# Two activations placed behind copies, a table loaded in three parts, and two small loads placed later, in an S4D and spectral-filter kernel

## The chip, the cores and the metric

One core of a Trainium2 chip runs the whole kernel. The metric is the device time of one execution in microseconds; the median of several runs counts. Data lie in the chip's HBM; a transfer (DMA) brings them into the on-chip memory of 128 partitions, and matmuls write to PSUM, from where another engine has to copy them away. The engines are TensorE (PE; its weight loads appear as PEld), VectorE (DVE), ScalarE (ACT), GpSimd (POOL) and SyncE (SP), which here only issues transfers. Each works through its own queue of instructions.

## The reference

The input x has 2048 positions and 640 channels. Branch a is a state-space convolution over the positions, branch b a two-dimensional spectral filter, and a gate worked out from x mixes them.

```python
dt = exp(log_dt)                                   # one per channel
A = -exp(log_A_real) + 1j * A_imag                 # 640 x 128
C = (C_real + 1j * C_imag) * dt[:, None]
P = exp((A * dt[:, None])[:, :, None] * pos)
K = 2.0 * einsum("dn,dnl->dl", C, P).real          # a filter per channel
y = irfft(rfft(u_t, 2 * L) * rfft(K, 2 * L))[:, :, :L]
a = y + u * D_skip
X = rfft2(x) * (w_r + 1j * w_i)
b = irfft2(X)
g = sigmoid((x * gate_w).sum(-1))
out = g * a + (1 - g) * b
```

## The kernel before

All Fourier transforms over the positions are two steps of small matmuls. The **first step** (`stage1`) takes 32-point transforms: four channels' matmuls fill one PSUM buffer, and a copy brings it to a tile `t1`. The **second step** (`stage2`) multiplies `t1` with a table `w2` (33 matrices of 128 x 128) and fills one PSUM buffer per pair of frequencies; a copy brings that to `ut`. There are three PSUM buffers for both steps, and four `ut` tiles, each of which holds two copies of the second step and is then written to a buffer `u_d` in HBM (line 455).

Phase A (`phase_a`) does this for u in four quarters of the channels (`c` 0 to 3). Each quarter is loaded in two halves (line 412, three buffers), the first step runs over 2 x 20 columns, and between come small matmuls with the gate's weights `z` (lines 417, 442). Then the second step makes 17 copies. The copies (line 405) are ScalarE's until a marked matmul, `T.pin`, in quarter 1; after it they are VectorE's.

Phase P (`phase_p`) makes the parameters of the filter K. From log_dt it works out dt on tiny tiles. From C it takes the larger and the smaller of the two parts, their quotient `q` (lines 308 to 313), its Arctan on ScalarE (line 316), the phase `ph` out of that (317 to 329), and from `q` again the logarithm of the magnitude, with Ln on ScalarE (line 338) and what follows (339 to 342). The activation Exp of line 344 and what GpSimd makes of it give the decay; GpSimd also makes the angle `th`. Each result is split into three bf16 parts (`parts`), and these are written to two buffers in HBM: `par_d[0]` for angles and phases, with constant rows from the table `t_one` beside them, and `par_d[1]` for decays and magnitudes.

Phase B (`phase_b`) builds K in 40 steps. It reads the parameters back (line 660), multiplies `par_d[1]`'s with a constant `rm` (line 670, in the helper `mags`, followed by Exp), `par_d[0]`'s with `rp` (line 680, followed by Sin), and sums the products over the 128 states (line 723). Its first matmuls may not stand before `T.pin`.

What sets the order: the phases are generators that yield from time to time. `body` advances phase P to its first yield, phase A to its first, then phase P to its end, then phase A until `T.pin` exists; from there `merge` interleaves phase A, and after it the spectral branch and phase C (`ga`), with phase B (`gl`). The instructions are then put in order, engine by engine, by a planner that goes by this order and by when it takes an instruction to be ready; so an instruction can stand ahead of one that was traced earlier. `tc.issue_after(x)` makes what is traced inside it stand behind x on x's engine, without a wait on another engine. The planner also puts the waits between engines. Transfers are issued from the queue of the engine that is named: `nc.sync` is SP, `G` is GpSimd, `nc.scalar` is ScalarE.

The skip weights `T.dsk` (D_skip, line 423, four rows) are first used in phase C, at line 782.

Of the kernel before, what the change touches and what calls it, by code (L numbers as in the profile page):

```python
# [12 lines left out]
AF = mybir.ActivationFunctionType  # L13
# [11 lines left out]
NP = 33  # L25
# [170 lines left out]
def body(tc, A, out):  # L196
    nc = tc.nc
    T = Ctx()
    with ExitStack() as top:
        dram = top.enter_context(tc.tile_pool(name="dram", bufs=1, space=DRAM))  # L200
        T.u_d = dram.tile([4, 128, 17, 2, 160], F32, name="u_d")
        T.s3e_d = dram.tile([4, 32, 64, 160], F32, name="s3e_d")
        T.s3_d = dram.tile([4, 64, 64, 160], F32, name="s3_d")
        T.k_d = dram.tile([4, 128, 40, 64], F32, name="k_d")
        T.par_d = [dram.tile([8, 4, 32, 5, N], BF, name="par_d0"), dram.tile([8, 16, 6, 5, N], BF, name="par_d1")]
        cst = top.enter_context(tc.tile_pool(name="cst", bufs=1))
        c1 = cst.tile([128, A["t_c1"].shape[1]], F32, name="c1")
        for x in (slice(0, 256), slice(256, c1.shape[1])):
            nc.scalar.dma_start(c1[:, x], A["t_c1"][:, x])
        o = 0  # L210

        def take(n):
            nonlocal o
            o += n
            return c1[:, o - n:o]

        T.e1 = [take(128), take(128)]
        T.e3, T.e3e, T.id, T.one = take(64), take(128), take(128), take(32)
        T.sg = [take(1), take(1)]
        T.hpi = take(1)  # L220
        T.w2 = cst.tile([128, NP, 128], F32, name="w2")
        T.gate = cst.tile([128, 2, 16], F32, name="gate")
        T.dsk = cst.tile([128, 4, 40], F32, name="dsk")
        T.pin = None
        with ExitStack() as cctx:
            def left():
                with ExitStack() as ctx:
                    T.bc = ctx.enter_context(tc.tile_pool(name="b_c", reuse_waits="tile", bufs=1))
                    T.rm = T.bc.tile([96, 1536], BF, name="rm")
                    T.rp = T.bc.tile([128, 2560], BF, name="rp")  # L230
                    yield from phase_p(tc, A, T)
                    yield 0.0
                    yield from phase_b(tc, A, T, ctx)

            ga, gl = chain(phase_a(tc, A, T), phase_c(tc, A, T, cctx)), left()
            next(gl)
            next(ga)
            next(gl)
            while T.pin is None:
                next(ga)  # L240
            merge((194.0, ga), (76.8, gl))
            phase_d(tc, A, T, cctx, out)


def phase_p(tc, A, T):

    nc = tc.nc
    V, G, S = nc.vector, nc.gpsimd, nc.scalar
    with ExitStack() as ctx:
# [11 lines left out]
        lar, ai, cr, ci = tn("lar"), tn("ai"), tn("cr"), tn("ci")  # L261
        for t, nm in ((cr, "cr_l"), (ci, "ci_l"), (ai, "ai_l"), (lar, "la_l")):
            nc.sync.dma_start(t[:, :, :], A[nm])
        nc.sync.dma_start(T.par_d[0][:, :, 24:32], A["t_one"])

        x, kf, r, h = t5("x"), t5("kf"), t5("r"), t5("h")
        V.tensor_scalar(out=x[:, :], in0=ld[:, :], scalar1=-87.0, scalar2=88.0, op0=ALU.max, op1=ALU.min)
        V.tensor_scalar(out=kf[:, :], in0=x[:, :], scalar1=1.0 / LN2, scalar2=MAGIC, op0=ALU.mult, op1=ALU.add)
# [31 lines left out]
        with tc.issue_after(ins.ins):  # L300
            G.dma_start(T.rm[:, :], A["t_rm"])
            G.dma_start(T.rp[:, :], A["t_rp"])
        G.tensor_tensor(out=th[:, :, :], in0=th[:, :, :], in1=w2[:, :, :], op=ALU.subtract)
        G.tensor_scalar(out=th[:, :, :], in0=th[:, :, :], scalar1=0.5, scalar2=-0.5, op0=ALU.min, op1=ALU.max)

# [7 lines left out]
        V.tensor_tensor(out=q[:, :, :], in0=q[:, :, :], in1=w[:, :, :], op=ALU.mult)  # L313
        V.tensor_tensor(out=ab[:, :, :], in0=ab[:, :, :], in1=ar[:, :, :], op=ALU.is_gt)
        ph, y = tn("ph"), tn("y")
        S.activation(ph[:, :, :], q[:, :, :], AF.Arctan)
        V.tensor_scalar(out=ph[:, :, :], in0=ph[:, :, :], scalar1=1.0 / (2 * math.pi), scalar2=None, op0=ALU.mult)
        V.tensor_scalar(out=y[:, :, :], in0=ph[:, :, :], scalar1=-2.0, scalar2=0.25, op0=ALU.mult, op1=ALU.add)
        V.tensor_tensor(out=y[:, :, :], in0=y[:, :, :], in1=ab[:, :, :], op=ALU.mult)
# [15 lines left out]
        V.tensor_tensor(out=w[:, :, :], in0=ff, in1=ff, op=ALU.mult)  # L335
        V.tensor_tensor(out=q[:, :, :], in0=q[:, :, :], in1=q[:, :, :], op=ALU.mult)
        V.scalar_tensor_tensor(out=q[:, :, :], in0=q[:, :, :], scalar=1.0, in1=w[:, :, :], op0=ALU.add, op1=ALU.mult)
        S.activation(q[:, :, :], q[:, :, :], AF.Ln)
        V.tensor_scalar(out=y[:, :, :], in0=ex[:, :, :], scalar1=-126.0, scalar2=LN2, op0=ALU.add, op1=ALU.mult)
        V.scalar_tensor_tensor(out=q[:, :, :], in0=q[:, :, :], scalar=0.5, in1=y[:, :, :], op0=ALU.mult, op1=ALU.add)  # L340
        V.tensor_tensor(out=q[:, :, :], in0=q[:, :, :], in1=bc(ld), op=ALU.add)
# [33 lines left out]
def phase_a(tc, A, T):  # L375
    nc = tc.nc
    V, G, S, P = nc.vector, nc.gpsimd, nc.scalar, nc.tensor

    with ExitStack() as ctx:
        def pool(name, bufs):  # L380
            return ctx.enter_context(tc.tile_pool(name=name, side="right", reuse_waits="tile", bufs=bufs))


        au = pool("a_u", 3)
        ap = pool("a_p", 2)
        ta = [pool("a_t0", 1)]
        a1 = pool("a_1", 4)
        ta.append(pool("a_t1", 1))
        ac = pool("a_c", 1)
        ps = ctx.enter_context(tc.tile_pool(name="a_ps", side="right", reuse_waits="tile", bufs=3, space=PSUM))  # L390
        gw = ac.tile([128, 4, 40], F32, name="gw")
        lg = ac.tile([128, 8, 64], F32, name="lg")
        lr = ac.tile([128, 64], F32, name="lr")


        V.memset(lg[:, :, :], 0.0)
        V.memset(T.dsk[:, :, :], 0.0)
        z = lg.rearrange("p x a -> p (x a)")
        p = ps.tile([128, 512], F32, tag="ps", name="p_w")
        for _ in range(2):  # L400
            P.matmul(p[:, :], z[:, 0:128], z, start=True, stop=True)

        def copy(dst, src):

            (V.tensor_copy if T.pin else S.copy)(dst, src)  # L405

        us = []

        def load(c, h):
            us.append(au.tile([128, 20, 64], F32, tag="u", name="u"))  # L410
            for q0, q1 in ((0, 6), (6, 20)) if c + h == 0 else ((0, 20),):
                nc.sync.dma_start(us[-1][:, q0:q1, :], A["u_l"][c, :, 20 * h + q0:20 * h + q1])

        def weights(c, h):

            z = ap.tile([128, 20, 32], F32, tag="z", name="z")
            G.tensor_tensor(out=z[:, :, :], in0=T.one.unsqueeze(1).broadcast_to([128, 20, 32]),  # L417
                            in1=gw[:, c, 20 * h:20 * h + 20].unsqueeze(2).broadcast_to([128, 20, 32]), op=ALU.mult)
            return z

        nc.scalar.dma_start(gw[:, :, :], A["gw_l"])
        for r in range(4):
            nc.sync.dma_start(T.dsk[32 * r:32 * r + 1, :, :], A["ds_l"][r:r + 1])
        load(0, 0)
        load(0, 1)
        zs = [weights(0, 0), weights(0, 1)]
        for c in range(4):
            t1 = ta[c % 2].tile([128, 16, 160, 2], F32, tag="t1", name="t1")
            t1v = t1.rearrange("p x d y -> p d x y")
            for h in range(2):  # L430
                u, z = us.pop(0), zs.pop(0)
                if c + h == 0:
                    yield 0.0
                    nc.sync.dma_start(T.w2[:, :, :], A["t_w2"].rearrange("p (k m) -> p k m", m=128))
                if c < 3:
                    load(c + 1, h)
                yield from stage1(nc, ps, T.e1, lambda q: u[:, q, :], 20, t1v[:, 80 * h:80 * h + 80], copy)

                p = ps.tile([128, 64], F32, tag="ps", name="p_g")
                for q in range(20):  # L440
                    x = 32 * (q % 4)
                    P.matmul(p[x:x + 32, :], z[:, q, :], u[:, q, :], start=q < 4, stop=q > 15)
                    if q % 4 == 3:
                        yield 0.15
                S.copy(lg[:, 2 * c + h, :], p[:, :])
                if c < 3:
                    zs.append(weights(c + 1, h))
            for pr in range(0, 17, 2) if c < 3 else (8, 10, 12, 14, 16, 0, 2, 4, 6):
                n = min(2, 17 - pr)
                nl = 128 if pr < 16 else 64  # L450
                ut = a1.tile([128, 2, 2, 160], F32, tag="ut", name="ut")
                for i in range(n):
                    pv, ins = stage2(nc, ps, T.w2, t1, pr + i, 1)
                    copy(ut[:nl, i:i + 1], pv)
                nc.sync.dma_start(T.u_d[c, :nl, pr:pr + n], ut[:nl, :n])
                if (c, pr) == (1, 8):
                    T.pin = ins
                yield 0.55 * n


        p = ps.tile([128, 64], F32, tag="ps", name="p_g")
        V.tensor_reduce(out=lr[:, :], in_=lg.rearrange("p x a -> p a x"), axis=mybir.AxisListType.X, op=ALU.add)
        for r in range(4):
            P.matmul(p[32 * r:32 * r + 32, :], T.one, lr[:, :], start=True, stop=True)
        for r, x in enumerate((slice(31, 15, -1), slice(32, 48), slice(15, None, -1), slice(48, 64))):
            V.tensor_copy(T.gate[32 * r:32 * r + 32, 0, :], p[32 * r:32 * r + 32, x])
# [556 lines left out]
```

## Time and profile before

| what | value |
|---|---|
| median of three runs | 594.21 us (591.97 to 594.76) |
| the profiled execution | 594.76 us, span 592.8 us |
| TensorE busy | 544.7 us, 92% |
| VectorE busy | 459.0 us, 77% |
| ScalarE busy | 324.8 us, 55% |
| GpSimd busy | 263.0 us, 44% |
| moved by DMA | 100.94 MB, mean 170 GB/s |

The span is the time from the first to the last instruction of the profiled execution; the run's own time is a little longer. A row of the timeline reads: start and duration in us, engine, source line, operation, output and inputs, form, count; in brackets the time for which the engine was idle before it and what ended that. Rows of equal instructions are merged, and their duration is that of all of them. An engine's name with a q (SPq) is its queue's own instruction, such as the issue of a transfer. A row of waits reads: engine, operand and line, what it waited for, and then the total in us, the number of waits, and the longest. A float32 matmul appears as two records. A row of transfers gives the operand, queue, count, size of one, and the time from the end of its issue to its landing. A row of windows gives the stretch, its length, the busy time of PE, PEld, DVE, ACT and POOL with the number of instructions, the clock granted to TensorE as a share of full speed, the DMA engines' busy share and GB/s.

### The profile page before, as it was taken

How to read it: one execution, taken by the hardware profiler on the slowest of the kernel's cores; microseconds unless marked ns; L12 is line 12 of the kernel's file. 1: busy time of each engine (PE TensorE's matmuls, PEld its weight loads, DVE VectorE, ACT ScalarE, POOL GpSimd, SP SyncE). 2: the span in 40 equal slices, each digit the busy share in tenths (PEclk: the TensorE clock that was granted, in tenths of full speed). 3: DMA queues.
4: the chain of work that ended last, by engine and by line, in shares of the span. 5: the costliest groups of instructions: out<-in, count | busy, mean ns of one | idle time of the engine just before them, and what ended most of it. 6: DMA issues, size and time to landing. Idle time of an engine off the chain costs nothing. (4 is left out here: it accounts for less than half of the span.)

```text
span 592.8 us, 16600 instructions
## 1 busy us (share of the span) xinstructions
PE 544.7 (92%) x7084; PEld 400.4 (68%) x7084; DVE 459.0 (77%) x713; ACT 324.8 (55%) x579; POOL 263.0 (44%) x267
## 2 busy tenths in 40 slices
PE   9388899999979999999899999899889999999975
PEld 7278556757665666675667675665778978887751
DVE  5993379688779989979969968958469596785955
ACT  4346666465826776777587878487632423232120
POOL 3972055053345616336406316217335256647533
PEclk9879999999979999999799999999999999999989
DMA  8757512317532340234140223012695989989787
GB/s 270 301 212 232 186 55 79 137 26 270 216 101 73 93 151 11 69 127 156 58 120 11 66 69 121 24 50 91 229 389 177 336 283 335 336 250 315 262 255 272
DMA packets 47409, 100.94 MB, mean 170 GB/s; under 512 B 3460, under 2 KB 32920, under 8 KB 45544
## 3 DMA queue, kind: packets, MB, share of 16 engines
q1 hardware_dynamic: 24936, 68.06, 33.4%
q10 hardware_dynamic: 20080, 22.52, 12.0%
q0 software_dynamic: 2320, 9.31, 4.6%
q8 instruction: 55, 0.90, 0.6%
q14 instruction: 18, 0.15, 0.1%
HBM read 60.55 MB, written 39.65 MB: 169 GB/s over the span
## 5 line engine op out<-in xcount | busy, mean ns | idle before, releaser
L370 PE MATMUL p_s<-t,w 128*64 128x160 f32 x1056 | 93.3, 316 | 14.8 <-ACT ut L405 8.7
L370 PEld LDWEIGHTS p_s<-t,w 128*64 128x64 f32 x1056 | 78.8, 140 | 25.3 <-ACT ut L405 9.5
L672 ACT ACTIVATE e<-p_e 128x512 f32<-128x512 f32 x120 | 68.8, 603 | 26.4 <-PE p_e L670 24.6
L709 POOL TENSOR_TENSOR y<-e,sc 128x512 f32<-128x512 f32 x40 | 51.8, 1295 | 62.6 <-ACT sc L694 35.9
L691 DVE TENSOR_SCALAR aq<-p_p 128x512 int32<-128x512 int32 x80 | 53.8, 684 | 22.5 <-PE p_p L680 22.1
L723 PEld LDWEIGHTS p_k<-x,y 128*32 128x32 f32 x2560 | 44.6, 111 | 36.5 <-issue 33.4
L589 PE MATMUL p_eo<-td,pmt 107*128 107x321 f32 x204 | 66.9, 442 | 0.3 <-ACT pmt L541 0.3
L680 PE MATMUL p_p<-rp,par 128*128 128x512 bf16 x240 | 65.6, 381 | 0.5 <-ACT sx L696 0.3
L723 PE MATMUL p_k<-x,y 128*32 128x64 f32 x2560 | 60.7, 225 | 1.2 <-POOL z L417 0.7
L358 ACT COPY t<-p_s 128x512 f32<-128x512 f32 x40 | 24.8, 624 | 64.7 <-PE p_s L357 45.2
L710 POOL TENSOR_TENSOR y<-e,sc 128x512 f32<-128x512 f32 x40 | 53.8, 1345 | 0.0
L706 DVE TENSOR_TENSOR x<-e,cx 128x1024 f32<-128x1024 f32 x40 | 48.5, 1212 | 2.4 <-ACT cx L697 2.4
L831 DVE TENSOR_TENSOR ma<-p_s,us 128x640 f32<-128x640 f32 (+1 forms) x36 | 28.2, 783 | 27.8 <-PE p_s L370 16.4
L589 PEld LDWEIGHTS p_eo<-td,pmt 107*128 107x128 f32 x204 | 36.9, 189 | 17.4 <-issue 4.3
L670 PE MATMUL p_e<-rm,par 96*128 96x512 bf16 x120 | 43.6, 386 | 5.0 <-ACT sx L696 3.7
L859 PE MATMUL p_i<-t,w 128*64 128x160 f32 x528 | 44.4, 304 | 4.0 <-POOL t L837 3.7
L357 PE MATMUL p_s<-c,kt 128*64 128x128 f32 x640 | 43.3, 274 | 3.4 <-POOL kt L782 2.1
L357 PEld LDWEIGHTS p_s<-c,kt 128*64 128x64 f32 x640 | 38.9, 136 | 10.4 <-issue 6.1
L357 PE MATMUL p_s<-c,u 128*64 128x128 f32 x640 | 43.0, 281 | 2.0 <-ACT ut L405 1.7
L859 PEld LDWEIGHTS p_i<-t,w 128*64 128x64 f32 x528 | 38.3, 139 | 8.4 <-POOL t L837 4.3
L357 PEld LDWEIGHTS p_s<-c,u 128*64 128x64 f32 x640 | 36.3, 139 | 11.3 <-issue 6.2
L837 POOL TENSOR_TENSOR t<-mb 64x320 f32<-64x320 f32 (+1 forms) x36 | 29.8, 828 | 28.3 <-DVE t L837 27.8
(157 smaller groups left out, 1069.0 us busy)
## 6 DMA issues: line engine op xcount, KB each, us to landing
u_d<-ut SPq DMA_DIRECT2D x32, 320.0 KB, 3.0
us<-u_d ACTq DMA_DIRECT2D x16, 640.0 KB, 6.5
s_d<-s ACTq DMA_DIRECT2D x15, 640.0 KB, 9.5
t<-s_d SPq DMA_DIRECT2D x14, 640.0 KB, 4.3
ww<-in_w_l SPq DMA_DIRECT2D x8, 642.0 KB, 3.8
ue<-u_d SPq DMA_DIRECT2D x8, 640.0 KB, 5.2
k_d<-kt SPq DMA_DIRECT2D x4, 1280.0 KB, 6.4
kt<-k_d SPq DMA_DIRECT2D x8, 640.0 KB, 6.4
```

What stands on the lines that cost most here:

```text
L357: nc.tensor.matmul(p[64 * ri:64 * ri + 64, j, :], src(i + j), e1[ri], start=True, stop=True)
L370: ins = nc.tensor.matmul(p[64 * j:64 * j + 64, i, 160 * ri:160 * ri + 160], w2[:, x, 64 * ri:64 * ri + 64], t1[:, x // 2 if x < 32 else K0 ...
L589: P.matmul(p[:, :E], st.pmt[:DC, c, w, j, :], tv[:DC, w, c, :], start=c == 0, stop=c == 2)
L670: P.matmul(p[:, :], pars[1][t], rm[:, c:c + 512], start=True, stop=True)
L672: st.exp = S.activation(ef[:, c:c + 512], p[:, :], AF.Exp)
L680: P.matmul(p[:, :], pars[0][t], w, start=i == 0, stop=i == 2)
L691: V.tensor_scalar(out=af[:, c:c + 512].bitcast(I32), in0=r.p[c][:, :].bitcast(I32), scalar1=0x7FFFFFFF, scalar2=None, op0=ALU.bitwise_and)
L706: V.tensor_tensor(out=x[:, 0].rearrange("p d (h j) -> p d h j", h=2), in0=e[:, :, 0:64].rearrange("p d (h j) -> p d h j", h=2), in1=cx.uns ...
L709: G.tensor_tensor(out=y[:, 1], in0=e[:, :, 64:96], in1=sc[:, 0], op=ALU.mult)
L710: G.tensor_tensor(out=y[:, 0], in0=e[:, :, 64:96], in1=sc[:, 1], op=ALU.mult)
L723: P.matmul(st.pb[32 * r:32 * r + 32, o, :], y[:, ri, 4 * qq + JR[r], :], x[:, ri, 4 * qq + JR[r], :], start=t % 2 + qq + 1 - ri == 0, stop ...
L859: T.mm = P.matmul(p[x:x + 64, i // 2, 160 * (i % 2):160 * (i % 2) + 160], T.w3[:, k0 + h + i, x:x + 64], t2[:, h + i, :], start=True, stop ...
```

## The change

- Arctan (line 316) is traced after six copies of the second step and stands behind the sixth on ScalarE; Ln (line 338) is traced after sixteen copies and stands behind the sixteenth. What phase P does after each of them is traced later with it. To that end, phase A keeps its copies of the second step in a list `T.cps`, phase P yields twice more, and `body` advances the two in turn.
- The table `w2` comes in three loads of eleven matrices each, in place of one.
- The four rows of skip weights are issued after the first load for quarter 1, in place of before the loads of quarter 0.
- The constant rows `t_one` go to `par_d[0]` from GpSimd's queue, behind the loads of `rm` and `rp`, in place of from SyncE's.

```diff
-        T.pin = None
+        T.pin, T.cps = None, []
...
             next(gl)
             next(ga)
+            for n in (6, 15):
+                next(gl)
+                while len(T.cps) < n:
+                    next(ga)
             next(gl)
             while T.pin is None:
                 next(ga)
...
             nc.sync.dma_start(t[:, :, :], A[nm])
-        nc.sync.dma_start(T.par_d[0][:, :, 24:32], A["t_one"])
...
             G.dma_start(T.rp[:, :], A["t_rp"])
+            G.dma_start(T.par_d[0][:, :, 24:32], A["t_one"])
...
-        S.activation(ph[:, :, :], q[:, :, :], AF.Arctan)
+        yield 0.0
+        with tc.issue_after(T.cps[-1].ins):
+            S.activation(ph[:, :, :], q[:, :, :], AF.Arctan)
...
-        S.activation(q[:, :, :], q[:, :, :], AF.Ln)
+        yield 0.0
+        with tc.issue_after(T.cps[-1].ins):
+            S.activation(q[:, :, :], q[:, :, :], AF.Ln)
...
-            (V.tensor_copy if T.pin else S.copy)(dst, src)
+            return (V.tensor_copy if T.pin else S.copy)(dst, src)
...
         nc.scalar.dma_start(gw[:, :, :], A["gw_l"])
-        for r in range(4):
-            nc.sync.dma_start(T.dsk[32 * r:32 * r + 1, :, :], A["ds_l"][r:r + 1])
         load(0, 0)
         load(0, 1)
...
                 if c + h == 0:
                     yield 0.0
-                    nc.sync.dma_start(T.w2[:, :, :], A["t_w2"].rearrange("p (k m) -> p k m", m=128))
+                    for x in range(0, NP, 11):
+                        nc.sync.dma_start(T.w2[:, x:x + 11, :], A["t_w2"].rearrange("p (k m) -> p k m", m=128)[:, x:x + 11, :])
                 if c < 3:
                     load(c + 1, h)
+                if c + h == 0:
+                    for r in range(4):
+                        nc.sync.dma_start(T.dsk[32 * r:32 * r + 1, :, :], A["ds_l"][r:r + 1])
...
                     pv, ins = stage2(nc, ps, T.w2, t1, pr + i, 1)
-                    copy(ut[:nl, i:i + 1], pv)
+                    T.cps.append(copy(ut[:nl, i:i + 1], pv))
```

## The prediction

> **What bounds the kernel now.** I read the page first.
>
> ```profile
> span 592.8 us, 16600 instructions
> PE 544.7 (92%) x7084; PEld 400.4 (68%) x7084; DVE 459.0 (77%) x713; ACT 324.8 (55%) x579; POOL 263.0 (44%) x267
> PE   9388899999979999999899999899889999999975
> ```
>
> TensorE is busy for 92% of the span, and its order is laid down in advance. So time is lost where TensorE stands still, and a stall taken out moves all that follows. The first hole is the second slice (14.8 to 29.6 us, three tenths busy), where the change works. Next come the waits of the first 64 us, for TensorE and ScalarE.
>
> ```profile
> PE p_s L370 <- ACT ut L405: 8.7, 2, 7.9
> PE p_s L370 <- DMA w<-in_t_w: 3.4, 1, 3.4
> ...
> ACT ph L316 <- DVE q L313: 5.2, 1, 5.2
> ACT q L338 <- DVE q L337: 4.9, 1, 4.9
> ```
>
> TensorE's second step (L370) waits 3.4 us for its table and 7.9 us for ScalarE's copies, while ScalarE waits 5.2 and 4.9 us for VectorE, at Arctan (L316) and Ln (L338). The timeline puts these in order.
>
> ```profile
> 1.63 1.71 SPq L423 DMA_DIRECT2D dsk<-in_ds_l  x4
> ...
> 6.99 1.25 SPq L264 DMA_DIRECT2D par_d<-in_t_one  x1
> ...
> 8.28 0.57 SPq L434 DMA_DIRECT2D w<-in_t_w  x1
> ...
> 11.66 1.43 DVE L308 TENSOR_SCALAR ar<-cr 128x640 int32<-128x640 int32 x1 [4.09 <-DMA cr<-in_cr_l]
> ...
> 16.36 0.77 PE L442 MATMUL p_g<-u,z 128*32 128x64 f32 x40
> ...
> 17.42 1.28 ACT L316 ACT_TABLE_LOAD   x1
> 17.48 0.73 POOL L301 DMA_DIRECT2D rm<-in_t_rm  x1
> ...
> 20.55 3.44 PE L370 MATMUL p_s<-t,w 128*64 128x160 f32 x24 [3.42 <-DMA w<-in_t_w]
> ...
> 22.53 1.33 DVE L313 TENSOR_TENSOR q<-q,w 128x640 f32<-128x640 f32 x1
> ...
> 23.90 0.74 ACT L316 ACTIVATE ph<-q 128x640 f32<-128x640 f32 x1 [5.20 <-DVE q L313]
> ...
> 28.75 2.01 DVE L337 SCALAR_TENSOR_TENSOR q<-q,w 128x640 f32<-128x640 f32 x1
> ...
> 30.79 0.74 ACT L338 ACTIVATE q<-q 128x640 f32<-128x640 f32 x1 [4.85 <-DVE q L337]
> 31.43 1.06 ACT L405 COPY ut<-p_s 128x320 f32<-128x320 f32 x3
> 31.89 8.30 PE L370 MATMUL p_s<-t,w 128*64 128x160 f32 x76 [7.91 <-ACT ut L405]
> ```
>
> One copy takes 8 of these records. The 24 records at 20.55 fill the three PSUM buffers by 24.0. Their copies stand behind Arctan and Ln and start only at 31.43.
>
> The second chain is the parameters'. VectorE works from 11.66 without a pause worth naming until the last part of the decay parameters is done. That part is written out, read back, and opens the first matmuls of the second stream (L670).
>
> ```profile
> 39.23 1.28 POOL L417 TENSOR_TENSOR z<-c,gw 128x640 f32<-128x640 f32 x1
> ...
> 41.70 0.95 ACT L405 COPY ut<-p_s 128x320 f32<-128x320 f32 x2 [0.19 <-PE p_s L370]
> ...
> 43.39 0.82 DVE L340 SCALAR_TENSOR_TENSOR q<-q,y 128x640 f32<-128x640 f32 x1
> ...
> 45.66 0.42 ACT L405 COPY ut<-p_s 64x320 f32<-64x320 f32 x1 [3.02 <-DMA u_d<-ut]
> ...
> 48.52 0.83 DVE L289 TENSOR_TENSOR parts<-q,parts 128x640 bf16<-128x640 f32 x1
> ...
> 49.64 0.54 POOL L291 DMA_DIRECT2D par_d<-parts  x1 [1.53 <-DVE parts L289]
> ...
> 54.92 6.46 PE L370 MATMUL p_s<-t,w 128*64 128x160 f32 x88
> ...
> 57.16 1.04 POOL L660 DMA_DIRECT2D par<-par_d  x2 [4.56 <-DMA par_d<-parts]
> ...
> 62.93 0.60 PE L670 MATMUL p_e<-rm,par 96*128 96x512 bf16 x2
> ```
>
> The issues of this chain have these times to landing (one write at 49.6, one at 47.5; one read at 57.2, one at 76.4; last a load of u issued at about 17.5):
>
> ```profile
> par_d<-parts POOLq DMA_DIRECT2D x1, 480.0 KB, 7.0
> ...
> par_d<-parts POOLq DMA_DIRECT2D x1, 480.0 KB, 3.5
> ...
> par<-par_d POOLq DMA_DIRECT2D x1, 120.0 KB, 4.8
> ...
> par<-par_d POOLq DMA_DIRECT2D x1, 120.0 KB, 2.6
> ...
> u<-in_u_l SPq DMA_DIRECT2D x1, 640.0 KB, 11.9
> ```
>
> The reader is to see how closely the two chains meet: 49.64 + 0.54 + 7.0 = 57.2 for the write, 57.16 + 0.5 + 4.8 = 62.5 for the read, and the first L670 stands at 62.93, right behind the matmul that opens this stream. Anything that the copies gain beyond 0.4 us is worth nothing to L670 unless the parameters also come sooner.
>
> **The change, part by part.**
>
> *Arctan and Ln behind the copies.* No instruction is added to ScalarE; the two move. Its queue behind Arctan holds the later copies, and for those TensorE waits. Stage 2 can start at 16.36 + 0.77 = 17.1 if its table is there. At the rate of 54.92 (88 records are 11 copies in 6.46 us, 0.59 each) six copies take 3.5 us, and the sixth ends at about 21.1. Then come a table load of 1.28 and Arctan, which still needs L313. That ended at 23.86; by the loads (below) I take 22.7, so Arctan ends at about 23.4. The 7th and 8th copies end at 24.4. The 9th needs a free output tile (there are four, two copies each), that is, the first write to u_d has to land. On SyncE's queue this write stands behind the load of u at 17.5, which landed at 17.5 + 0.3 + 11.9 = 29.7. With the loads a little sooner I take 28.5. Eight copies at 0.48 (the row at 41.70 has two in 0.95) end at 32.3, Ln with its table (1.28 + 0.74) at 34.3, the 17th copy at 34.8. Before, that was 45.66 + 0.42 = 46.1, so the first stream gains 11.3 us here. It would then reach the place of L670 at 62.93 - 11.3 = 51.6. Bounds: 8 if the first write lands 3 us later still; 15 if the ring costs nothing, for then ten copies end at 28.2, Ln is held by L337 to about 30.5, and the 17th copy ends at 31.
>
> VectorE doesn't lose by it: between L313 (to 23.86) and the end of L337 (30.76) it has 6.9 us of work that needs no Arctan, and Ln is first needed at 43.39, nine microseconds after my 34.3. Without that cover each microsecond of lateness would be paid in full by the parameters.
>
> *Skip weights.* Four issues, 1.71 us on SyncE, leave the place ahead of most of u and of the parameters and go behind the third load of u. There the other loads of u and the writes to u_d queue behind them; these wait for earlier tiles and bytes anyway, so I take 0 (bounds 0 and 1.71). Ahead, cr can land up to 1.71 us sooner. The DMA engines are already nearly full then, so I take 1.2 (bounds 0 and 1.71).
>
> *Constant rows.* 1.25 us leave SyncE and come to GpSimd behind two loads; the nearest row is 0.73 there. The rows are needed only by the read of the other parameter set, later. GpSimd's work on z (1.28, now at 39.23) is traced ahead of the parameters' parts, so it may also move into VectorE's busy time. I charge 0.6 for both (bounds 0 and 0.73 + 1.28 = 2.0).
>
> *The table in three loads.* Two more issues of 0.57, 1.1 us on SyncE ahead of u loads that nobody waits for yet: 0 (bounds 0 and 1.1). The 2112 KB went at about 400 GB/s (next fence, first row), so a third takes 1.8 us and the first lands 3.6 us before the last. Even without an earlier start that is 20.55 - 3.6 = 17.0, when stage 1 ends. The wait of 3.42 us goes; it is inside the 11.3.
>
> *What is late next.* The parameters: VectorE's last part ended at 48.52 + 0.83 = 49.35, now 49.35 - 1.2 + 0.6 = 48.75. Write: 0.3 + 0.54 + 3.5 = 53.1, with the uncontended landing, because u has been loaded long before. Read: 0.54 + 2.6 = 56.2, and with L670's own 0.2 it starts at 56.4. Both bounds of the landings: 56.4, and with 7.0 and 4.8 again 62.1. With all the small terms at their ends it is 55.3 to 64.7. I take the short ones, since the stream that filled the queue at 49.6 will have halted. So TensorE stands for 56.4 - 51.6 = 4.8 us, and the gain up to here is 62.93 - 56.4 = **6.5 us**, not 11.3.
>
> *The cost of standing.* After the stall of 7.9 us TensorE came back slow.
>
> ```profile
> 10.00:15.00 5.00, 4.94 (x116) 4.44 (x112) 3.30 (x3) 2.81 (x6) 2.82 (x3) 1.00 1.07 420
> ...
> 31.90:35.10 3.20, 3.20 (x24) 2.81 (x26) 3.10 (x4) 1.44 (x4) 3.20 (x4) 0.50 0.45 171
> 35.10:38.30 3.20, 3.20 (x30) 2.83 (x30) 3.17 (x2) 1.28 (x4) 3.20 (x3) 0.60 0.36 136
> 38.30:42.00 3.70, 3.70 (x56) 3.70 (x53) 3.52 (x4) 2.86 (x7) 2.19 (x3) 1.00 0.87 337
> ...
> 62.90:69.30 6.40, 5.32 (x43) 3.01 (x42) 2.86 (x6) 4.45 (x7) 0.00 (x0) 1.00 0.45 171
> ```
>
> The granted clock was 0.50 and 0.60 for 6.4 us, and 54 records took what 97 take at the rate of the fourth row: 2.8 us lost. Behind L670 the same could happen. TensorE is busy there for 5.32 of 6.4 us, so about 1 us of it falls into waits. I charge 2.0 (bounds 0 and 2.8). The Trainium skill ("TensorE: Matmul & The Clock Gate", Part 1) says that the clock halves after an idle window of about 3.4 us and returns after some 3.4 us of sustained work. By that figure alone the loss would be an estimated 1.7 us in place of 2.0; the rows here show a slow stretch almost twice as long. It speaks against the change all the same, since a stall that is only moved buys a cold clock at its new place.
>
> **Sum.** 6.5 - 2.0 = 4.5 us. The profiled execution took 594.76 (span 592.8, the rest around it) and was the slowest of the three; 594.76 - 4.5 = 590.3. The median is 0.55 below, so 589.7.
>
> **Rivals.**
>
> *The parameters don't hold TensorE.* If the order puts more of the first stream ahead of L670, the stall is filled and the whole 11.3 stays: 594.21 - 11.3 = 582.9. For it: the order isn't simply that of the code (z at 39.23 is traced after the parameters' write of 49.64, yet runs before it). Against: in the old order L670 stands directly behind its opening matmul.
>
> *The landings stay long.* With 7.0 and 4.8 again L670 starts at 62.1, a gain of 0.8 which a cold clock takes back: 593.4 to 595.4, no change.
>
> *Ln comes late* (slower). The place is the 16th copy. It ended at 41.70 + 0.95 = 42.65 before; if the ring of four output tiles, whose writes now queue behind the loads, holds the copies there still, Ln ends at 42.65 + 1.28 + 0.74 = 44.7, 1.3 us after L340 wants it, and L670 moves to 62.93 + 1.3 = 64.2, with 2.0 for the clock: 594.21 + 3.3 = 597.5. It decides once the 16th copy ends later than 41.4. Against: the copies would need 9 us more of waits than I found.
>
> **Chances.** Forecast 0.50, with a range of its own from 586.6 to 593.0 (a gain of 7.6 is 62.93 - 55.3 with no loss of clock; 1.2 is half way to the long landings, 59.2, less 2.5 for the clock); filled stall 0.21; long landings 0.15; late Ln 0.14. What the measurement can tell from no change is 0.5%, 3.0 us. Faster: 0.21 and four fifths of the forecast, 0.61. Same: the rest of the forecast and most of the long landings, 0.24. Slower: 0.15. The range goes from below the filled stall, 581.5, to the late Ln, 597.
>
> **What would show it.** Step by step: TensorE's L370 starts by 17.5 with no wait for the table; three copies no longer start together after Ln; the 9th copy waits for u_d; L670's first matmul stands near 56 and waits for the read of par; granted clock near 0.5 behind it. Wrong would be: L670 near 51 or near 63, VectorE waiting for Arctan or Ln, or a loss that arises after 100 us, where the order of later work may have shifted.

## The result, and the profile after

The changed kernel takes 599.24 us (median of 20 runs), the kernel before 591.49 us (median of 20 runs beside it). The ratio is 1.0127 with a 95% interval of 1.0099 to 1.0155: **slower by about 7.5 us**, where 4.5 us faster was forecast. The first lines of the changed kernel's page, with the slices of 15 us for TensorE's busy tenths and the clock granted to it:

```profile
span 597.6 us, 16599 instructions
...
PE   9794899999979999999899999899889999999985
...
PEclk9998589999979999999899999999999999999979
```

The hole in the second slice is nearly gone. A new one stands in the fourth (45 to 60 us), and the clock is down in the fifth (60 to 75 us). Behind that the page all but repeats the one before. The timeline of the changed kernel shows the front (start, duration, engine, line, operation, idle before and its releaser):

```profile
16.95 5.32 PE L377 MATMUL p_s<-t,w 128*64 128x160 f32 x72
...
22.60 0.74 ACT L321 ACTIVATE ph<-q 128x640 f32<-128x640 f32 x1 [0.26 <-DVE q L316]
...
26.40 1.76 ACT L412 COPY ut<-p_s 128x320 f32<-128x320 f32 x4 [2.42 <-DMA u_d<-ut]
...
31.73 0.74 ACT L345 ACTIVATE q<-q 128x640 f32<-128x640 f32 x1
...
32.38 0.40 ACT L412 COPY ut<-p_s 64x320 f32<-64x320 f32 x1
```

The second step (L377) starts at 16.95 with no wait for its table, Arctan waits 0.26 us in place of 5.20, Ln not at all, and the 17th copy ends at 32.78 in place of 46.08. Up to here the change did what it was to do, and 13.3 us are won. The same timeline, further on:

```profile
33.36 0.98 POOL L289 CAST parts<-lar 128x640 bf16<-128x640 f32 x1
...
44.64 0.66 POOL L293 DMA_DIRECT2D par_d<-parts  x1 [8.35 <-DVE parts L291]
45.30 0.57 POOL L296 DMA_DIRECT2D par_d<-parts  x1
45.63 0.83 DVE L291 TENSOR_TENSOR parts<-ph,parts 128x640 bf16<-128x640 f32 x1
...
47.33 1.42 POOL L291 TENSOR_TENSOR lar<-lar,parts 128x640 f32<-128x640 f32 x1
...
51.80 1.39 POOL L291 TENSOR_TENSOR parts<-lar,parts 128x640 bf16<-128x640 f32 x1
...
54.82 0.55 POOL L293 DMA_DIRECT2D par_d<-parts  x1
...
59.16 1.05 POOL L669 DMA_DIRECT2D par<-par_d  x2 [3.25 <-DMA par_d<-parts]
61.56 0.13 PEld L679 LDWEIGHTS <-par 96*128 96x128 bf16 x2 [7.90 <-DMA par<-par_d]
61.57 1.03 PE L679 MATMUL p_e<-rm,par 96*128 96x512 bf16 x2 [7.59 <-DMA par<-par_d]
```

VectorE is done with its last part at 46.5, 2.9 us earlier than before. But on GpSimd the write of the magnitude's parts (L293, which needs VectorE) now stands *ahead of* the rest of the decay's parts (`lar`). GpSimd waits for it for 8.35 us with its own work behind it. Work on `z` and a read of the other parameter set stand among that work too, so the decay's write goes out only at 54.82. The read of both follows at 59.16, and the first matmul of the second stream stands at 61.57 after a TensorE wait of 7.59 us.

TensorE's own order has changed as well, first in the changed kernel, then in the one before:

```profile
41.62 6.46 PE L377 MATMUL p_s<-t,w 128*64 128x160 f32 x88
48.88 2.49 PE L377 MATMUL p_s<-t,w 128*64 128x160 f32 x32 [0.80 <-ACT ut L412]
53.19 0.78 PE L377 MATMUL p_s<-t,w 128*64 128x160 f32 x6 [1.82 <-DVE ut L412]
...
65.33 0.61 PE L679 MATMUL p_e<-rm,par 96*128 96x512 bf16 x1
65.87 0.70 PE L364 MATMUL p_s<-c,u 128*64 128x128 f32 x4
```

```profile
62.20 0.79 PE L370 MATMUL p_s<-t,w 128*64 128x160 f32 x8 [0.82 <-ACT ut L405]
...
66.62 0.60 PE L670 MATMUL p_e<-rm,par 96*128 96x512 bf16 x2
67.16 1.36 PE L370 MATMUL p_s<-t,w 128*64 128x160 f32 x16
```

The changed kernel runs 88 + 32 + 6 = 126 second-step records ahead of the second stream, the kernel before 88 + 8 = 96. So 30 records, an estimated 2.2 us at the rate of 88 in 6.46, have moved ahead of it. Behind that, one matmul of the second stream (`p_e`) alternates with two to six records of the first for some 12 us, where the kernel before has mostly pairs and blocks of 10 and 16. The windows of the changed kernel from there (length; busy time of PE, PEld, DVE, ACT, POOL with counts; granted clock; DMA share; GB/s):

```profile
54.00:61.50 7.50, 0.00 (x0) 0.00 (x0) 0.49 (x1) 0.00 (x0) 2.73 (x5) 0.59 0.56 193
61.50:65.00 3.50, 3.11 (x11) 1.27 (x11) 0.97 (x2) 2.56 (x4) 0.00 (x0) 0.50 0.09 33
65.00:70.00 5.00, 5.00 (x23) 1.94 (x22) 0.00 (x0) 2.73 (x5) 0.00 (x0) 0.50 0.19 59
70.00:75.00 5.00, 5.00 (x24) 1.93 (x23) 1.26 (x2) 1.88 (x5) 0.00 (x0) 0.50 0.00 0
75.00:80.00 5.00, 5.00 (x34) 2.86 (x35) 0.84 (x3) 2.26 (x4) 0.00 (x0) 0.58 0.00 0
80.00:85.00 5.00, 5.00 (x76) 2.68 (x74) 3.00 (x5) 4.41 (x7) 2.02 (x3) 1.00 0.28 49
```

One such row of the kernel before, with the same kinds of matmul in its own order:

```profile
70.00:75.00 5.00, 5.00 (x61) 3.20 (x62) 2.42 (x4) 3.17 (x6) 0.00 (x0) 1.00 0.23 74
```

At half the clock 24 matmul records pass in 5 us, at full clock and in the old order 61. The half clock lasts some 17 us. A good mark for the end of this stretch is the first product matmul (`p_k`), which has the same TensorE work ahead of it in both orders, from the start of the kernel on. In the kernel before and in the changed one:

```profile
84.86 0.32 PE L723 MATMUL p_k<-x,y 128*32 128x64 f32 x8
```

```profile
88.99 0.32 PE L732 MATMUL p_k<-x,y 128*32 128x64 f32 x8
```

From the second stream's first matmul to this mark it is 84.86 - 62.93 = 21.9 us before and 88.99 - 61.57 = 27.4 us after. That is 5.5 us more for 30 records less, so half clock and new order together cost an estimated 5.5 + 2.2 = 7.7 us. At its first `p_e` the changed kernel was 1.4 us earlier and those 2.2 us of work further on, 3.6 us ahead; at the mark it is 4.1 us behind. Matched one by one, TensorE's instructions keep this distance of 4.1 us from 75 to 410 us. The difference between these 4.1 and the 7.5 us of the medians lies, at least in part, in the profile of before that served as the base, as the fifth experiment shows.

### The profile page after: what moved, and what is told of

Read it like the earlier page. It is cut to its first block, busy times and chain, and to the rows that moved or that the text cites. A ratio compares the mean times of both kernels' runs of the same rounds, so it can differ in the third digit from the quotient of the medians.

```text
span 597.6 us, 16599 instructions
## 1 busy us (share of the span) xinstructions
PE 550.9 (92%) x7084; PEld 401.1 (67%) x7084; DVE 455.5 (76%) x713; ACT 325.3 (54%) x579; POOL 264.1 (44%) x268
## 5 line engine op out<-in xcount | busy, mean ns | idle before, releaser
L377 PE MATMUL p_s<-t,w 128*64 128x160 f32 x1056 | 89.1, 306 | 8.8 <-ACT ut L412 4.1
L377 PEld LDWEIGHTS p_s<-t,w 128*64 128x64 f32 x1056 | 75.5, 135 | 17.4 <-ACT ut L412 5.0
L679 PE MATMUL p_e<-rm,par 96*128 96x512 bf16 x120 | 47.3, 412 | 11.8 <-DMA par<-par_d 7.6
L364 PE MATMUL p_s<-c,u 128*64 128x128 f32 x640 | 48.9, 296 | 0.6 <-ACT ut L412 0.6
L868 PE MATMUL p_i<-t,w 128*64 128x160 f32 x528 | 45.6, 311 | 2.9 <-POOL t L846 2.6
L364 PEld LDWEIGHTS p_s<-c,u 128*64 128x64 f32 x640 | 39.0, 146 | 13.8 <-issue 10.1
L669 POOL DMA_DIRECT2D par<-par_d x16 | 9.0, 565 | 76.7 <-PE p_e L679 64.5
```

The source lines that it names most:

```text
L364: nc.tensor.matmul(p[64 * ri:64 * ri + 64, j, :], src(i + j), e1[ri], start=True, stop=True)
L377: ins = nc.tensor.matmul(p[64 * j:64 * j + 64, i, 160 * ri:160 * ri + 160], w2[:, x, 64 * ri:64 * ri + 64], t1[:, x // 2 if x < 32 else K0 ...
L679: P.matmul(p[:, :], pars[1][t], rm[:, c:c + 512], start=True, stop=True)
L868: T.mm = P.matmul(p[x:x + 64, i // 2, 160 * (i % 2):160 * (i % 2) + 160], T.w3[:, k0 + h + i, x:x + 64], t2[:, h + i, :], start=True, stop ...
```

## The experiments

The theory: the front's gain is worth nothing because the second stream waits for its parameters; these come later than before, as GpSimd stands at a write ahead of the decay's work; and behind the wait TensorE runs at half its clock. Rivals: the loads or the placing of the activations cost by themselves; the loss arises later; the two profiles differ by chance.

| kernel | first p_e | first p_k | between | time us | ratio to before (95%) |
|---|---|---|---|---|---|
| before, first profile | 62.93 | 84.86 | 21.9 | 591.49 | 1 |
| before, second profile (5) | 58.39 | 80.33 | 21.9 | 592.00 (one run) | |
| changed | 61.57 | 88.99 | 27.4 | 599.24 | 1.0127 (1.0099 to 1.0155) |
| changed, second profile (6) | 62.25 | 89.67 | 27.4 | 602.27 (one run) | |
| loads only (1) | 66.26 | 88.20 | 21.9 | 598.41 | 1.0132 (1.0084 to 1.0180) |
| activations only (2) | 57.94 | 81.78 | 23.8 | 594.47 | 1.0062 (1.0032 to 1.0092) |
| decay first (3) | 59.65 | 85.55 | 25.9 | 595.07 | 1.0060 (1.0029 to 1.0091) |
| idle matmuls (4) | 61.24 | 83.18 | 21.9 | 598.08 | 1.0104 (1.0042 to 1.0167) |
| idle matmuls again (10) | 59.99 | 81.93 | 21.9 | 594.05 | 1.0081 (1.0047 to 1.0116) |
| decay first, idle matmuls (11) | 59.76 | 81.70 | 21.9 | 594.06 | 1.0053 (1.0015 to 1.0091) |
| before, later place (9) | 67.53 | | | 580.69 | 0.9857 (0.9807 to 0.9907) |
| decay first, later place (7) | 61.70 | | | 574.98 | 0.9727 (0.9697 to 0.9758) |
| activations only, later place (8) | 61.60 | | | 575.14 | 0.9739 (0.9713 to 0.9764) |
| decay first, latest place (12) | 62.79 | | | 571.95 | 0.9655 (0.9594 to 0.9715) |

"First p_e" is the start of the second stream's first matmul in the profile of that kernel; "between" is left empty where the second stream starts at another place of the first. In the changed kernel 30 second-step records fewer stand between the two, with the decay first 14 fewer; the other numbers in that column are for the work and the order of before. Times are medians of up to 20 runs, ratios are against the kernel before on the same chip, so a ratio can differ a little from the quotient of two medians of this table.

**1. The loads alone.** The changed kernel with Arctan, Ln and the advancing of the phases as before.

```diff
-            for n in (6, 15):
-                next(gl)
-                while len(T.cps) < n:
-                    next(ga)
...
-        with tc.issue_after(T.cps[-1].ins):
-            S.activation(ph[:, :, :], q[:, :, :], AF.Arctan)
+        S.activation(ph[:, :, :], q[:, :, :], AF.Arctan)
```

> Only the changes of the loads; Arctan and Ln stand as in the kernel before. Theory (the parameters' chain and the clock behind a stall set the start of the second stream): here the planner puts GpSimd's write of the magnitude's parts (it waits for VectorE until about 42 us) ahead of most of the angle's and the decay's parts, so the decay's write goes out at 52 to 58, the first matmul of the second stream stands at 60 to 67, TensorE waits 5 us or more ahead of it and then has half the clock: 3 to 10 us slower than before. Rival (placing Arctan and Ln behind the copies is what costs): within 3 us of before, or faster.

1.0132, and the first p_e at 66.26. Its timeline for GpSimd, and its waits of TensorE in the first 90 us:

```profile
35.40 0.62 POOL L289 DMA_DIRECT2D par_d<-parts  x1 [14.11 <-DVE parts L287]
...
53.22 0.60 POOL L289 DMA_DIRECT2D par_d<-parts  x1
...
59.03 1.04 POOL L661 DMA_DIRECT2D par<-par_d  x2 [2.85 <-DMA par_d<-parts]
```

```profile
PE p_g L443 <- POOL z L416: 13.1, 1, 13.1
```

GpSimd stands even longer at the same write, 14.11 us, and here the gate's weights `z` are among the work behind it. TensorE waits 13.1 us for them, earlier than expected and for another tile; by the second stream its clock is back. So the loads alone cost as much as the whole change (1.0127). Of the loads moved only the constant rows went to GpSimd's queue; which of the moves turned its order was not tried.

**2. The activations alone.** The kernel before with Arctan and Ln placed as in the change; all loads as before.

```diff
+            for n in (6, 15):
+                next(gl)
+                while len(T.cps) < n:
+                    next(ga)
...
+        with tc.issue_after(T.cps[-1].ins):
+            S.activation(ph[:, :, :], q[:, :, :], AF.Arctan)
...
+        with tc.issue_after(T.cps[-1].ins):
+            S.activation(q[:, :, :], q[:, :, :], AF.Ln)
```

> Only Arctan and Ln behind the 6th and 16th copy; all loads as before. Theory: GpSimd's queue keeps the decay's parts ahead of its waits, so its last write isn't held; first matmul of the second stream at 57 to 62, between 4 us faster and 4 us slower than before, by whether the clock falls. Rival (placing the activations costs by itself): 6 us or more slower than before.

1.0062, as the theory has it. GpSimd's decay work is ahead of its waits here, the first p_e stands at 57.94 and waits 7.1 us. TensorE's order is that of the kernel before. Its rows behind the stall, and the window of the half clock:

```profile
61.08 1.86 PE L378 MATMUL p_s<-t,w 128*64 128x160 f32 x10
62.87 1.03 PE L678 MATMUL p_e<-rm,par 96*128 96x512 bf16 x2
63.84 1.60 PE L378 MATMUL p_s<-t,w 128*64 128x160 f32 x16
```

```profile
57.90:64.40 6.50, 6.13 (x25) 2.84 (x27) 0.98 (x2) 3.85 (x6) 0.00 (x0) 0.50 0.03 9
```

Here the half clock ends at 64.4 and costs 1.9 us (23.8 in place of 21.9). At the mark the kernel is 81.78 - 80.33 = 1.4 us behind the second profile of before.

**3. The decay first.** The four lines of the decay are traced behind the angle's parts.

```diff
         parts(th, 0, 0, G)
+        S.activation(lar[:, :, :], lar[:, :, :], AF.Exp)
+        G.tensor_tensor(out=lar[:, :, :], in0=lar[:, :, :], in1=bc(dtn), op=ALU.mult)
+        G.tensor_scalar(out=lar[:, :, :], in0=lar[:, :, :], scalar1=-1.0e6, scalar2=None, op0=ALU.max)
+        parts(lar, 1, 0, G)
...
-        parts(lar, 1, 0, G)
```

> The changed kernel with the decay's Exp and GpSimd's work on it traced behind the angle's parts, so that GpSimd no longer waits for VectorE ahead of them. Theory: the wait of 8.4 us is gone, the first matmul of the second stream stands at 55 to 58 in place of 61.6, and the kernel is 4 to 9 us faster than the changed one (590 to 595). Rival (the loss is elsewhere): within 2 us of the changed one, 597 to 601.

595.07, some 4 us faster than the changed kernel and just outside the 590 to 595 expected; the first p_e at 59.65, not 55 to 58. Its timeline for GpSimd:

```profile
47.84 0.56 POOL L296 DMA_DIRECT2D par_d<-parts  x1 [9.10 <-DVE parts L291]
48.42 1.42 POOL L291 TENSOR_TENSOR parts<-lar,parts 128x640 bf16<-128x640 f32 x1
49.77 1.13 POOL L293 DMA_DIRECT2D par_d<-parts  x2
...
56.98 1.04 POOL L669 DMA_DIRECT2D par<-par_d  x2 [2.36 <-DMA par_d<-parts]
```

All but one of the decay's parts are now ahead of the wait, and the last write goes out 4.5 us earlier, at 50.3. But it lands 6.1 us after the start of its issue, and the read goes out only at 56.98. The DMA engines' share is 1.02 from 49 to 54 us: three parameter writes of 480 KB stand close together there, and the first stream's writes to u_d came forward with the copies into the same time. Which of the two delays the landing was not tried.

**4. Idle matmuls through the wait.** The changed kernel with 14 matmuls that nobody reads, ahead of the second stream.

```diff
+                if (c, pr) == (1, 10):
+                    p = ps.tile([128, 512], F32, tag="ps", name="p_w")
+                    for _ in range(14):
+                        P.matmul(p[:, :], T.e1[0], T.c1[:, 0:512], start=True, stop=True)
```

> The changed kernel with 14 matmuls of 512 columns, whose result nobody reads, on TensorE ahead of the first matmul of the second stream. Theory (the half clock behind the stall costs 5 to 6 us): that matmul stays at 61 to 63, the granted clock is 1.00 behind it, and the time is 592 to 595. Rival (the parameters' lateness alone, or the order after 80 us): 598 or more, whatever the clock.

The first p_e stays at 61.24, the clock is 1.00 in every window behind it, and the distance to the first p_k is 21.9 again. But the run doesn't part the clock from the order: with the idle matmuls in place TensorE's work stands in the order of the kernel before once more, with the 30 records behind the first p_e and the blocks of 10 and 16. What it shows is that half clock and new order together make the 5.5 us. And the time, 598.08, missed the expectation and fell where the rival had it; its interval is wide, 1.0042 to 1.0167. In the profiled run 4.5 us went to a wait at the very end, one that other profiles have with 0 to 2.9 us. So it was run again as the tenth.

**5 and 6. Both kernels once more, for a second profile.**

> The kernel before once more, for a second profile. Theory: up to 90 us the times repeat the first profile's within 1 us; what differs between two executions of one kernel arises at TensorE's later stalls (about 165, 290, 380, 450 us and at the end), by steps of 1 to 3 us. Rival: the first part itself varies by 2 us or more.

> The changed kernel once more, for a second profile. Theory: first matmul of the second stream again at 60 to 63 with half the clock for 10 us or more behind it; the first product matmul (p_k) 3 us or more later than in the kernel before. Rival: the clock comes back within 7 us and the loss of the first profile was chance.

The changed kernel repeats itself from the second stream on: 62.25, 27.4 us to the mark, half clock until 79.9. Its first stream came later, so that TensorE waited 4.93 us there, not 7.59. The kernel before doesn't: its first p_e stands at 58.39, 4.5 us earlier than in the profile on which the forecast was made. The rival was right there. TensorE and GpSimd in this second profile:

```profile
30.18 10.37 PE L370 MATMUL p_s<-t,w 128*64 128x160 f32 x107 [5.15 <-ACT ut L405]
```

```profile
49.36 0.54 POOL L291 DMA_DIRECT2D par_d<-parts  x1 [1.53 <-DVE parts L289]
...
53.10 1.04 POOL L660 DMA_DIRECT2D par<-par_d  x2 [0.47 <-issue]
```

```profile
par<-par_d POOLq DMA_DIRECT2D x1, 120.0 KB, 4.9
```

The stall behind Arctan and Ln was 5.15 us in place of 7.91. The write landed in 3.2 us in place of 7.0 (a load of u was issued 0.1 us behind it in the first profile and 1.7 us behind it in this one), so the read could go at 53.10. That read took 4.9 us and landed at 53.10 + 4.9 = 58.0, just ahead of the first p_e, which had no wait of its own. So the two chains meet here as closely as in the first profile, only 4.5 us earlier, and of the 13.3 us won at the front 9.4 are left against it (the 88 records start at 51.01 there, at 41.62 in the changed kernel). Against this profile the changed kernel is 88.99 - 80.33 = 8.7 us late at the mark: 61.57 - 58.39 = 3.2 up to the first p_e and 5.5 behind it. That lies within the measured 5.9 to 9.2 us (0.99 to 1.55% of 591.49).

**10. The idle matmuls again.**

> The kernel with 14 idle matmuls once more, because its six runs gave a wide interval. Theory: first matmul of the second stream at 61 to 62, and from there to the first product matmul 22 us as in the kernel before, 5 us less than in the changed one; time 2 to 5 us above the kernel before. Rival: 7 us or more above it again, the same as the changed kernel, so that the clock explains nothing of the total.

594.05, 2.9 us above the kernel before by the medians and 4.8 us by the ratio, as expected; the first p_k at 81.93, 1.6 us behind the second profile of before. The total agrees with the theory but doesn't prove it: the interval, 1.0047 to 1.0116, overlaps that of the changed kernel.

**11. Both repairs.** The third and fourth together, with 11 idle matmuls.

```diff
-                    for _ in range(14):
+                    for _ in range(11):
```

> Both repairs at once: the decay's work ahead of GpSimd's wait, and 11 idle matmuls ahead of the second stream. Theory: first matmul of the second stream at 58.5 to 60.5, warm clock behind it, first product matmul at 80.5 to 82.5: within 2.5 us of the kernel before. Rival: 4 us or more above it.

594.06, 1.0053 (1.0015 to 1.0091): 2.9 us above before, a little more than the theory allowed and less than the rival. At the mark it is 1.4 us behind the second profile of before; the rest lies within the interval. At the mark it is also 85.55 - 81.70 = 3.9 us ahead of the third experiment, of which the totals show no more than 1.0 us, so a distance at the mark is not yet one at the end. With both losses repaired the 8 us that the first stream was ahead at 45 us are worth nothing: TensorE spends them on idle matmuls.

**7. A later place for the second stream.** The third experiment's kernel, in which the second stream may start behind the gate matmuls of quarter 2's first half, with the weight of phase A in the merge lowered by the work that has gone ahead.

```diff
-                if (c, pr) == (1, 8):
-                    T.pin = ins
...
-                    P.matmul(p[x:x + 32, :], z[:, q, :], u[:, q, :], start=q < 4, stop=q > 15)
+                    ins = P.matmul(p[x:x + 32, :], z[:, q, :], u[:, q, :], start=q < 4, stop=q > 15)
+                    if (c, h, q) == (2, 0, 19):
+                        T.pin = ins
...
-            merge((194.0, ga), (76.8, gl))
+            merge((184.6, ga), (76.8, gl))
```

> The changed kernel with the decay's work as in the earlier experiment, and the second stream's first matmul behind the gate matmuls of the first half of quarter 2 (some 10 us of TensorE work later) in place of behind the 10th copy of quarter 1; the merge's weight is lowered by the work that has gone ahead. Theory: TensorE stands less than 2 us ahead of that matmul, the clock stays at 1.00, and the 10 to 12 us that the copies gained are kept: 579 to 585. Rival (what the front gains is given back later in any case): 590 or more.

574.98, faster than expected. The wait was still 2.57 us, and the clock was down from 64 to 70 us. TensorE now has useful work ahead of the parameters.

**8. The same place, with the activations alone.**

> Arctan and Ln behind the copies alone (all loads as in the kernel before), with the same later place of the second stream's first matmul. Theory: as the previous one, since without the loads the copies had gained as much at 45 us: within 2 us of it, 580 to 586. Rival (the loads are what makes the gain): 4 us or more slower than it.

575.14, the same within the intervals: here the changes of the loads and the decay's new place, which the seventh has and this one lacks, add nothing that can be seen.

**9. The control: the same place in the kernel before.**

> The kernel before with nothing but the later place of the second stream's first matmul and the lowered weight of the merge: the control for the two fast versions. Theory (the copies' gain of about 10 us is only kept where TensorE has work ahead of the parameters): without the change this kernel keeps its early stalls, so it lies between: 580 to 587. Rival (the later place alone makes the whole gain, and the change adds nothing): 573 to 577.

580.69 (0.9857), between. The later place with its merge weight alone is worth 1.4%, and with Arctan and Ln behind the copies 2.6 to 2.7%. So about half of what these two versions gain comes from placing the activations, and the later place gives the other half without it. Why the later place is better wasn't taken apart.

**12. A still later place.** Behind both halves, (2, 1, 19), with the weight lowered again.

```diff
-                    if (c, h, q) == (2, 0, 19):
+                    if (c, h, q) == (2, 1, 19):
...
-            merge((184.6, ga), (76.8, gl))
+            merge((179.0, ga), (76.8, gl))
```

> As the first fast version, with the second stream's first matmul behind both halves of quarter 2's first step (5.6 us of TensorE work later still). Theory: no wait for the parameters and no cold clock are left, so 1 to 3 us faster than the first fast version (575): 571 to 575. Rival (the second stream now starts too late, and ends late against the first): 577 or more.

571.95 (0.9655), the best version. TensorE in its profile:

```profile
60.71 0.77 PE L451 MATMUL p_g<-u,z 128*32 128x64 f32 x40
61.50 1.36 PE L377 MATMUL p_s<-t,w 128*64 128x160 f32 x16
62.79 0.61 PE L679 MATMUL p_e<-rm,par 96*128 96x512 bf16 x2
```

No wait stands ahead of the second stream, and the granted clock is 1.00 in every window from 45 to 75 us.

## Why the prediction was wrong

- *Arctan and Ln behind the copies*: right. The wait of the 9th copy for u_d came (it ended at 26.4, forecast 28.5), the 17th copy ended at 32.8 (forecast 34.8), and VectorE lost nothing; its last parts were even done at 46.5, forecast 48.75.
- *What is late next*: right in kind, the parameters hold the second stream and TensorE stands. The step that failed is the sum behind it, "Write: 0.3 + 0.54 + 3.5 = 53.1". It let the write follow VectorE's last part, as before. In the new order the decay's parts are the last, because GpSimd's queue waits for VectorE ahead of them; their write goes out at 54.82, and the first p_e stands at 61.57 in place of 56.4. The prediction listed what GpSimd takes on, and didn't ask what would stand behind its waits once the tracing order was another. TensorE stood 7.59 us, not 4.8, although it reached the wait later, at 53.98 and not 51.6, with 30 more records done.
- The landings in that sum were nearly right for the changed kernel: the decay's write landed in 3.8 us (3.5 taken), the read in 2.3 (2.6 taken). With the order repaired (third experiment) the write took 6.1. The view counts these times from the start of an issue, not from its end. The write's 0.54 can still stand for the time from its landing to the read (59.16 is 0.5 us behind 54.82 + 3.8). The read's 0.54 and L670's 0.2 were too much, since the first p_e stands at 61.57, right behind 59.16 + 2.3.
- *The cost of standing*: right in kind, but the term of 2.0 us (upper bound 2.8) came to 5.5 between the marks in both profiles, with 30 records less there, an estimated 7.7. For the old order it was right: the second experiment lost 1.9. The change also gave TensorE another order behind the stall, which the prediction didn't expect, and there half the clock lasted some 17 us.
- *The base*: the profile of before had its first p_e at 62.93, a second one at 58.39. Counted from there even 56.4 would have gained 2.0 us, which the clock's 2.0 would have taken.
- *The rivals*: "the landings stay long" has nearly the right start (62.1, measured 61.57), but by luck: the landings were short, and the write was late. "Ln comes late" was wrong, since Ln had run by 32.5. That the order would put more of the first stream ahead of the second came true for 30 records, which was far too little to fill the stall; made so by hand, in the seventh and twelfth experiments, it gave the gain that this rival named, and more, of which about half needs no change of the front (ninth).

## What to carry to other kernels

A stall that is filled moves the wait to whatever arrives next; look up when that arrives, and give the engine work until then, or the gain is spent standing and paid for again by a cold (halved) clock. Price that clock in the order that will stand behind the new stall: 2.0 us were right for the old order, and the new one cost far more. When the tracing order changes, read every in-order queue again for a wait that has slipped ahead of work which others need, also on engines that the edit doesn't name. And take a second profile of the base before summing microseconds.

## What the runs showed of the hardware

Behind TensorE stalls of 7.0 to 7.6 us the granted clock stayed at 0.50 for very different times:

```profile
59.60:72.70 13.10, 12.73 (x56) 5.49 (x58) 2.65 (x5) 7.04 (x11) 0.00 (x0) 0.50 0.16 56
```

```profile
69.03 1.97 PE L364 MATMUL p_s<-c,u 128*64 128x128 f32 x14
```

```profile
61.50:79.20 17.70, 17.31 (x76) 7.40 (x78) 3.05 (x5) 9.38 (x15) 0.00 (x0) 0.50 0.07 23
```

```profile
76.04 1.54 PE L364 MATMUL p_s<-c,u 128*64 128x128 f32 x10
```

The first window and the row under it are the third experiment's, the second pair the changed kernel's; the second experiment's 6.5 us are shown there. TensorE's records leave hardly a gap in any of them. What differs is the order: the longer one `p_e` at a time alternates with two to six float32 records, the longer the clock stays down. In all three it came back 3.2 to 3.7 us after the start of the first run of ten or more equal float32 records (at 61.08, 69.03 and 76.04; the clock's ends are 64.4, 72.7 and 79.2). The Trainium skill ("TensorE: Matmul & The Clock Gate", Part 1) has the clock back after some 3.4 us of sustained work. Counted from the end of the stall none of these stretches agrees, nor do the 6.4 us of the prediction's rows. That short alternating runs hold the clock down is a reading of these three orders; no run changed the order alone.
